# Issuing the x loads of a window-attention kernel from the ACT queue instead of SyncE

## The chip, the core and the metric

The kernel runs on one core of a Trainium2 chip. The metric is device time in microseconds, median of several runs. A run counts as fast unless it is over 1.5% above the fastest run of the same kernel; comparisons below use fast runs only. Names: PE is TensorE's matmul stream, ACT is ScalarE, DVE VectorE, POOL GpSimd, SP SyncE, which in this kernel only issues transfers. The issue time of a transfer is how long its instruction holds the queue that issues it; the transfer lands when all its data has arrived.

## The reference

Forward and backward of shifted-window attention without the shift: the image (256 x 256 pixels, 384 channels, bf16) is cut into windows of 8 x 8 = 64 tokens. The outputs are the forward result and the gradients of x, wqkv and wo.

```python
qkv = xw @ wqkv                      # xw: windows x 64 x 384
p = softmax(einsum('bqc,bkc->bqk', q, k) * 384 ** -0.5)
o = einsum('bqk,bkc->bqc', p, v) @ wo
_out, _vjp = jax.vjp(_f, x, wqkv, wo)
_grads = _vjp(grad_out)
```

## The kernel before

The loop takes 128 steps. A step handles eight windows (`QUAD` = 4 pairs) and works on three groups of windows at once: the scores and the u, v projections of one, the z and y projections of the next, and `attend` of the one before. All PSUM banks (where TensorE's products are written) are one ring of eight, handed out in turn. SP issues, per step, four loads of x (96 KB each) and four DMA transposes: `dT` and `xT` (12 blocks of 128 x 128 each), `PS` (4 blocks) and `tok` (24 blocks). POOL issues the loads of grad_out (`dq`) and the stores.

```python
ring = ctx.enter_context(tc.tile_pool(name="ring", bufs=8, space=bass.MemoryType.PSUM))
...
def load(st):
    st["xq"] = xq = grp.tile([P, QUAD, C], BF16, tag="xq", name="xq", bufs=2 * GQ + 4)
    st["dq"] = dq = qp.tile([P, QUAD, C], BF16, tag="dq", name="dq", bufs=6)
    for t in range(QUAD):
        nc.sync.dma_start(out=xq[:, t, :], in_=windows(x, st, 2 * t))
        nc.gpsimd.dma_start(out=dq[:, t, :], in_=windows(grad_out, st, 2 * t))
...
def step(c, b, a, ahead):            # cut: only the order that matters
    B(scores); ...                   # PE: sd;  then u, v projections, copied by ACT
    ...                              # softmax on DVE and ACT
    for mo in range(CK):
        A(project, 0, mo)            # PE: z from dT;  ACT copies it
    B(soft, 5); B(turn)              # SP: transpose PS<-ps
    if ahead is not None:
        load(ahead)                  # SP: four x loads;  POOL: four dq loads
    filler(1)
    C_(attend, (0, 1))               # takes all eight banks: pu, po, po, pd, pd, pw, pu, pw
    for mo in range(CK):
        A(project, 1, mo)            # PE: y;  ACT copies it
    A(to_tokens)                     # SP: transpose tok<-yz
    filler(1)
    C_(attend, (2, 3))
```

Ahead of each step stands `load_turn`, in which SP issues `dT` and `xT` of the group two steps on; its x loads were issued in the step before.

Of the kernel before, what the change touches and what calls it, by code (L numbers as in the profile page):

```python
# [11 lines left out]
BF16 = mybir.dt.bfloat16  # L12
F32 = mybir.dt.float32

P = 128
WIN = 8
WT = WIN * WIN
QUAD = 4
# [4 lines left out]
def kernel(  # L23
# [21 lines left out]
    nc = tc.nc  # L45
    _, H, W, C = x.shape
# [6 lines left out]
    grp = ctx.enter_context(tc.tile_pool(name="grp", bufs=2 * GQ + 1))  # L53
# [53 lines left out]
    def windows(ap, st, first, count=2):  # L107
        row, col = st["at"]
        return ap[0, row + WIN * first:row + WIN * (first + count), col:col + WIN, :]

    LO, HI = slice(0, WT), slice(WT, P)
    OTHER = {0: HI, WT: LO}

    def load(st):
        st["xq"] = xq = grp.tile([P, QUAD, C], BF16, tag="xq", name="xq", bufs=2 * GQ + 4)
        st["dq"] = dq = qp.tile([P, QUAD, C], BF16, tag="dq", name="dq", bufs=6)
        for t in range(QUAD):
            nc.sync.dma_start(out=xq[:, t, :], in_=windows(x, st, 2 * t))
            nc.gpsimd.dma_start(out=dq[:, t, :], in_=windows(grad_out, st, 2 * t))  # L119

    def load_turn(st):
        xq, dq = st["xq"], st["dq"]
        st["xT"] = xT = qp.tile([P, QUAD, CK, P], BF16, tag="xT", name="xT", bufs=3)
        st["dT"] = dT = qp.tile([P, QUAD, CK, P], BF16, tag="dT", name="dT")
        for src, dst in ((dq, dT), (xq, xT)):
            k = G_ON_PE if src is dq else 0
            if k < QUAD:
                nc.sync.dma_start_transpose(out=dst[:, k:].rearrange("p t m k -> p (t m) k"),
                                            in_=src[:, k:].rearrange("p t c -> p (t c)"))
# [49 lines left out]
    def over_k(ap, n=P):  # L179
        return ap.unsqueeze(2).broadcast_to([n, QUAD, WT])  # L180

    def soft(st, step):
        sd = st["sd"]
        if step == 0:
# [111 lines left out]
    def gf_group(sts):  # L296
        n = len(sts) * QUAD
        for f in range(2):
            for ma in range(CK):
                pw = ring.tile([P, C], F32, tag="r", name="pg")  # L300
                for i in range(n):
                    st, t = sts[i // QUAD], i % QUAD
                    product(pw[:], st["xq"][:, t, ma * P:(ma + 1) * P], st["UW"[f] + "q"][:, t, :], i == 0, i == n - 1)
                nc.vector.tensor_tensor(out=GF_acc[:, f, ma, :], in0=pw[:], in1=GF_acc[:, f, ma, :], op=ALU.add)  # L304
                yield

    def filler(n):
        while n and fill:
            try:
                next(fill[0])  # L310
                n -= 1
            except StopIteration:
                fill.pop(0)

    def step(c, b, a, ahead):


        def on(st):
            return (lambda f, *r: f(st, *r)) if st is not None else (lambda f, *r: None)
        C_, B, A = on(c), on(b), on(a)  # L320
        B(scores)
        B(soft, 0)
        B(uv, 0, 0)
        B(uv, 0, 1)
        B(soft, 1)
        B(uv, 1, 0)
        B(uv, 1, 1)
        B(soft, 2)
        B(soft, 3)
        B(uv, 2, 0)  # L330
        B(uv, 2, 1)
        for t in range(QUAD):
            A(grad_turn, t)
        B(uv, 3, 0)
        B(uv, 3, 1)
        B(soft, 4)
        for mo in range(CK):
            A(project, 0, mo)
        B(soft, 5)
        B(turn)  # L340
        if ahead is not None:
            load(ahead)
        filler(1)
        C_(attend, (0, 1))
        split[0] = True
        for mo in range(CK):
            A(project, 1, mo)
        A(to_tokens)
        filler(1)
        split[0] = ALL  # L350
        C_(attend, (2, 3))
# [4 lines left out]
    sts = [{"at": q, "i": i} for i, q in enumerate(quads)]  # L356
    n = len(sts)
    AHEAD = 3
    with tc.manual_schedule(engines=MANUAL):
        for i in range(min(AHEAD, n)):  # L360
            load(sts[i])
            if i < AHEAD - 1:
                load_turn(sts[i])
        held = []
        get = lambda i: sts[i] if 0 <= i < n else None
        for i in range(-1, n + 1):
            if AHEAD - 1 <= i + AHEAD - 1 < n:
                load_turn(sts[i + AHEAD - 1])
            step(get(i - 1), get(i), get(i + 1), get(i + AHEAD) if i >= 0 else None)
            if i > 0:  # L370
                held.append(sts[i - 1])
                sts[i - 1] = None
            if held and (len(held) == GQ or i == n):
                fill.append(gf_group(held))
                held = []
        split[0] = False
        filler(1 << 30)
# [62 lines left out]
```

## Time and profile before

| | before |
|---|---|
| median of 3 runs | 2007.22 us (1998.82 to 2007.71) |
| profiled span | 1997.5 us, granted clock 1.000 |
| TensorE busy | 99% |
| step of the loop | 15.2 us, 128 of them |

The lines that carry the reading stand in the prediction. The source-line views of the two longest-lived things on SP, the x loads and tok: count, then min/median/max of the issue in ns.

```profile
L118 SPq DMA_DIRECT2D xq<-in_x_dram x512: 575/600/2127, 1.2 to 1927.9; - x171
```
```profile
L167 SPq DMA_TRANSPOSE tok<-yz x128: 3862/4819/6547, 26.4 to 1951.7; - x128
```

Second, the DMA queues of the page: packets, MB, share of 16 engines. q1 is SP's, q0 POOL's, q10 ACT's, which is empty but for one load.

```profile
q1 hardware_dynamic: 943312, 270.60, 81.2%
q0 software_dynamic: 98304, 151.39, 31.1%
...
q10 hardware_dynamic: 400, 0.29, 0.0%
```

### The profile page before, as it was taken

The page shows a single profiled execution, that of the slowest core. Times are in us where ns is not written, and L with a number is a line of the kernel's source. Part 1 is how long each engine was busy: PE and PEld are TensorE (multiplying, and loading weights), DVE is VectorE, ACT ScalarE, POOL GpSimd, SP SyncE. Part 2 cuts the span into 40 slices and gives each one's busy share as a digit, 9 for nine tenths or more (in the row PEclk, how much of TensorE's full clock was granted, in tenths as well). Part 3 has the DMA queues.
Part 4 walks back from the last instruction along what each step waited for, and adds up shares of the span by engine and source line. Part 5 has one row for each costly group of instructions (what it writes and reads, how often), then busy time and mean ns, then how long its engine had stood idle before and what let it go on. Part 6 is the DMA issues. An engine that isn't in the chain of part 4 may idle for free. (4 is left out here: it accounts for less than half of the span.)

```text
span 1997.5 us, 52374 instructions
## 1 busy us (share of the span) xinstructions
PE 1967.7 (99%) x19418; PEld 1192.8 (60%) x19418; DVE 1317.2 (66%) x2979; ACT 1405.4 (70%) x3213; POOL 1122.9 (56%) x2054
## 2 busy tenths in 40 slices
PE   8899999999999999999999999999999999999998
PEld 4456656665666666566566656666665566566655
DVE  5666666666666666666666666666666666666666
ACT  5776767677777767777776777677776777776773
POOL 3555555565555556555655555565555556555643
PEclk9999999999999999999999999999999999999999
DMA  9999999999999999999999999999999999999993
GB/s 201 211 217 223 208 213 215 224 215 221 216 218 223 210 213 223 219 219 208 227 210 223 219 211 213 223 223 215 215 214 214 212 217 213 223 211 222 217 206 96
DMA packets 1042272, 425.62 MB, mean 213 GB/s; under 512 B 925792, under 2 KB 1016672, under 8 KB 1042016
## 3 DMA queue, kind: packets, MB, share of 16 engines
q1 hardware_dynamic: 943312, 270.60, 81.2%
q0 software_dynamic: 98304, 151.39, 31.1%
q8 instruction: 152, 2.49, 0.6%
q14 instruction: 104, 0.85, 0.1%
q10 hardware_dynamic: 400, 0.29, 0.0%
HBM read 101.84 MB, written 101.84 MB: 102 GB/s over the span
## 5 line engine op out<-in xcount | busy, mean ns | idle before, releaser
L292 POOL DMA_DIRECT2D out_dram<-o x256 | 139.2, 544 | 707.4 <-ACT o L264 697.4
L264 ACT CAST o<-po 128x384 bf16<-128x384 f32 x512 | 220.4, 482 | 370.0 <-PE pu L253 355.2
L304 DVE TENSOR_TENSOR GF_acc<-pg,GF_acc 128x384 f32<-128x384 f32 x258 | 144.0, 558 | 495.0 <-PE pg L145 343.8
L147 PEld LDWEIGHTS <-xT 128*128 128x128 bf16 x3072 | 291.8, 98 | 182.1
L147 PE MATMUL pj<-B_sb,xT 128*128 128x384 bf16 x1536 | 333.4, 326 | 0.0
L147 PE MATMUL pj<-AT_sb,xT 128*128 128x384 bf16 x1536 | 333.3, 326 | 0.0
L119 POOL DMA_DIRECT2D dq<-in_grad_out_dram x512 | 274.1, 547 | 66.0 <-DMA out_dram<-o 37.7
L147 PE MATMUL pj<-dT,BT_sb 128*128 128x512 bf16 x1152 | 269.7, 379 | 8.8 <-DMA dT<-dq 7.3
L145 PE MATMUL pj<-xT,A_sb 128*64 128x512 bf16 x2304 | 273.0, 380 | 1.6 <-DMA xT<-xq 1.6
L229 ACT CAST uq<-pj 128x384 bf16<-128x384 f32 x512 | 247.6, 484 | 30.6 <-PE pj L147 27.1
L229 ACT CAST vq<-pj 128x384 bf16<-128x384 f32 x512 | 249.9, 488 | 2.4 <-ACT uq L229 0.3
L145 PEld LDWEIGHTS <-xq 128*64 128x64 bf16 x3000 | 210.6, 110 | 46.3
L264 ACT CAST d<-pd 128x384 bf16<-128x384 f32 x512 | 225.2, 503 | 0.4 <-ACT o L264 0.2
L147 PEld LDWEIGHTS <-xq 128*128 128x128 bf16 x1572 | 153.6, 98 | 114.9 <-issue 0.3
L207 ACT COPY ps<-Pb 64x256 bf16<-64x256 bf16 x256 | 103.3, 403 | 149.6 <-DVE Pb L204 148.1
L163 ACT CAST yz<-pj 128x512 bf16<-128x512 f32 x384 | 206.3, 630 | 2.1 <-PE pj L145 1.8
L161 ACT CAST yz<-pj 128x512 bf16<-128x512 f32 x384 | 206.4, 639 | 1.1 <-ACT vq L229 0.7
L145 PEld LDWEIGHTS <-A_sb 128*64 128x64 bf16 x2304 | 155.7, 109 | 84.9 <-DMA xT<-xq 2.0
L147 PEld LDWEIGHTS <-BT_sb 128*128 128x128 bf16 x1152 | 111.5, 98 | 133.9 <-DMA dT<-dq 13.6
L147 PE MATMUL pg<-Uq,xq 128*128 128x384 bf16 x1032 | 181.6, 326 | 0.0
L258 PE MATMUL pd<-tok,ps 128*64 128x384 bf16 x1024 | 181.2, 344 | 0.0
L253 PE MATMUL pu<-xq,PS 64*64 64x384 bf16 x1024 | 174.9, 335 | 4.5 <-DMA PS<-ps 4.3
(67 smaller groups left out, 3382.2 us busy)
## 6 DMA issues: line engine op xcount, KB each, us to landing
xq<-in_x_dram SPq DMA_DIRECT2D x512, 96.0 KB, 4.0
dq<-in_grad_out_dram POOLq DMA_DIRECT2D x512, 96.0 KB, 3.9
out_dram<-o POOLq DMA_DIRECT2D x256, 96.0 KB, 4.2
out_dram<-o POOLq DMA_DIRECT2D x512, 48.0 KB, 4.4
out_dram<-d POOLq DMA_DIRECT2D x256, 96.0 KB, 4.4
out_dram<-d POOLq DMA_DIRECT2D x512, 48.0 KB, 4.4
dT<-dq SPq DMA_TRANSPOSE x128, 6.4
xT<-xq SPq DMA_TRANSPOSE x128, 6.7
```

The lines of the kernel that those rows point to most:

```text
L119: nc.gpsimd.dma_start(out=dq[:, t, :], in_=windows(grad_out, st, 2 * t))
L145: nc.tensor.matmul(out[h], lhsT=lhsT[:, h], rhs=rhs, start=start, stop=stop)
L147: nc.tensor.matmul(out, lhsT=lhsT, rhs=rhs, start=start, stop=stop)
L161: ENG[EV["z"][mo]](out=yz[:, mo, :, 0:4:3, :], in_=pj[:])
L163: ENG[EV["y"][mo]](out=yz[:, mo, :, 1:3, :], in_=pj[:])
L207: nc.scalar.copy(out=ps[h, :, w, :], in_=Pb[h, :, :])
L229: cp(out=dst[:, t, :], in_=pj[:])
L253: nc.tensor.matmul(at[o, :], lhsT=turned(st, lhs, t, h), rhs=st[rhs][h, t, :], **{"start": True, "stop": True, **fl})
L258: nc.tensor.matmul(pd[outer if w == 0 else 1 - outer][o, :], lhsT=st["ps"][:, t, w, :], rhs=st["tok"][:, :, t, w, :], **flags)
L264: nc.scalar.copy(out=sb[:], in_=src[outer][:])
L292: nc.gpsimd.dma_start(out=windows(dst, st, 2 * t0 + 1), in_=sb[:])
L304: nc.vector.tensor_tensor(out=GF_acc[:, f, ma, :], in0=pw[:], in1=GF_acc[:, f, ma, :], op=ALU.add)
```

## The change

SP is nearly full; ACT idles 2.14 us behind the copies of y. So the x loads of the loop move from SP to the ACT queue, behind those copies. The loads ahead of the loop stay on SP.

```diff
+    def load_x(st, queue):
+        for t in range(QUAD):
+            queue.dma_start(out=st["xq"][:, t, :], in_=windows(x, st, 2 * t))
+
     def load(st):
...
         for t in range(QUAD):
-            nc.sync.dma_start(out=xq[:, t, :], in_=windows(x, st, 2 * t))
             nc.gpsimd.dma_start(out=dq[:, t, :], in_=windows(grad_out, st, 2 * t))
...
             A(project, 1, mo)
+        if ahead is not None:
+            load_x(ahead, nc.scalar)
         A(to_tokens)
...
             load(sts[i])
+            load_x(sts[i], nc.sync)
```

More of the change, by code (lines that the diff above doesn't have):

```diff
@@ L112 @@
     OTHER = {0: HI, WT: LO}
+    def load_x(st, queue):
+        for t in range(QUAD):
+            queue.dma_start(out=st["xq"][:, t, :], in_=windows(x, st, 2 * t))
     def load(st):
-        st["xq"] = xq = grp.tile([P, QUAD, C], BF16, tag="xq", name="xq", bufs=2 * GQ + 4)
+        st["xq"] = grp.tile([P, QUAD, C], BF16, tag="xq", name="xq", bufs=2 * GQ + 4)
         st["dq"] = dq = qp.tile([P, QUAD, C], BF16, tag="dq", name="dq", bufs=6)
         for t in range(QUAD):
-            nc.sync.dma_start(out=xq[:, t, :], in_=windows(x, st, 2 * t))
             nc.gpsimd.dma_start(out=dq[:, t, :], in_=windows(grad_out, st, 2 * t))
```

## The prediction

> **What bounds the kernel now.** I read the busy table of the page first, then the waits of TensorE, then two steps of the timeline engine by engine, and last the instruction order of the changed kernel.
>
> ```profile
> PE 1967.7 (99%) x19418; PEld 1192.8 (60%) x19418; DVE 1317.2 (66%) x2979; ACT 1405.4 (70%) x3213; POOL 1122.9 (56%) x2054
> ...
> DMA  9999999999999999999999999999999999999993
> ...
> xq<-in_x_dram SPq DMA_DIRECT2D x512, 96.0 KB, 4.0
> ...
> wo_sb<-in_wo_dram ACTq DMA_DIRECT2D x1, 288.0 KB, 5.8
> ```
>
> TensorE has work in 99% of the span; only 30 us of 1997.5 are not covered, and the head and the tail of the kernel are in them. A busy TensorE could still be slow, so I checked the rate in the timeline: in the stretch of the u and v projections each group of three 128x384 products starts 0.49 us after the one before (1008.26, 1008.75, 1009.24), with nothing between. The scores start at 1007.55 and again at 1022.75: a step of the loop takes 15.2 us, there are 128, and 128 x 15.2 = 1946 us, almost the whole span. TensorE sets the pace. What could a better-fed TensorE win? Its own waits say:
>
> ```profile
> PE pj L147 <- DMA dT<-dq: 7.3, 6, 2.4
> ...
> PE pu L253 <- DMA PS<-ps: 4.3, 5, 1.6
> ...
> PE pj L145 <- DMA xT<-xq: 1.6, 1, 1.6
> ```
>
> The columns are total us, times, longest. These are the waits for the transposes that SyncE issues: 13.2 us in all, 0.7% of the run. That is the whole purse of a change that relieves SyncE, and by itself it rules out a gain of 2%.
>
> Second, SyncE is a full queue. Its timeline over one step:
>
> ```profile
> 1008.35 1.20 SPq L233 DMA_TRANSPOSE PS<-ps  x1
> 1009.59 2.79 SPq L118 DMA_DIRECT2D xq<-in_x_dram  x4
> 1012.49 5.45 SPq L167 DMA_TRANSPOSE tok<-yz  x1
> 1018.16 1.45 SPq L128 DMA_TRANSPOSE dT<-dq  x1
> 1019.79 3.23 SPq L128 DMA_TRANSPOSE xT<-xq  x1
> ```
>
> 1.20 + 2.79 + 5.45 + 1.45 + 3.23 = 14.1 us of 15.2, and the gaps are about 0.15 us each. Moreover it runs late: the y copies that tok waits for end at 1005.04 (the ACT row below), and tok is issued at 1012.49, 7.4 us later. Yet TensorE hardly feels it, as tok is not read until the step after next.
>
> Third, ScalarE (ACT), which is to take the loads. Its timeline around the new place:
>
> ```profile
> 1003.43 1.61 ACT L163 CAST yz<-pj 128x512 bf16<-128x512 f32 x3
> 1007.18 0.86 ACT L264 CAST o<-po 128x384 bf16<-128x384 f32 x2 [2.14 <-PE pu L253]
> 1007.93 0.88 ACT L264 CAST d<-pd 128x384 bf16<-128x384 f32 x2
> 1009.01 0.48 ACT L229 CAST uq<-pj 128x384 bf16<-128x384 f32 x1 [0.20 <-PE pj L147]
> ...
> 1014.83 1.61 ACT L161 CAST yz<-pj 128x512 bf16<-128x512 f32 x3
> ```
>
> Start, length, and in brackets the idle time before. Behind the three copies of y ACT idles 2.14 us, every step. The loads are put into exactly this hole, and the question of the whole case is whether they fit.
>
> **What the Trainium skill says.** "DMA: Bandwidth & Descriptors", section "Issuing engines are not separate DMA queues", says that DMAs run on the same 16 engines whoever issues them, and that issuing from several only saves sequencer time. So the change moves issue time, not transfer time; the DMA row, at 90% or more throughout, will not get lighter. "Perfetto Trace Analysis", section "DMA Instruction — HWDGE (DVE, Sync)", says that the block which generates descriptors is shared between sequencers, that an instruction waits for its lock, and that the profiled length includes this. If so, a load on ACT could wait behind a long transpose of SyncE. The trace has only one sign, and it is mild: at the very start w_sb on SyncE and wo_sb on ACT both begin at 0.74 us and take 0.45 and 0.49 us, side by side. No transpose was in flight then, so this trace doesn't decide it. The same page, section "DVE / Act Engine Instruction (TENSOR_ADD, Activation, etc)", says that the sequencer is free for the next instruction before the engine has executed the last; if that holds for an issue behind a copy, the loads start while the last y copy still runs. No row here shows it.
>
> **The change part by part.** The instruction order of both programs: TensorE, VectorE and GpSimd keep theirs; SyncE loses 125 groups of four loads (the first three groups stay); ACT gains these 500, after the third y copy and before the o copies.
>
> *Removed from SyncE:* one issue has a median of 0.600 us; four in a row took 2.58, 2.52, 3.27, 2.51, 2.98, 2.80, 2.69, 2.79 and 3.55 us in nine successive steps, 2.85 on average. SyncE then needs about 14.1 - 2.8 = 11.3 us of 15.2 and should catch up: tok would be issued right behind the y copies. The transposes' 13.2 us of waits should mostly go; I credit 5 to 10 us.
>
> *Added to ACT:* the issues. Undisturbed they are 4 x 0.6 = 2.4, with gaps about 2.5 (the best groups above); as they run on SyncE, 2.85. As they stand in the ACT stream, the o copies behind them wait.
>
> *What ACT may lose before TensorE notices.* The PSUM ring has eight banks and attend takes all eight in the order pu, po, po, pd, pd, pw, pu, pw. The scores take the first again, the first u projection the second, which is po's. That projection starts at 1008.26; the o copy that frees it runs 1007.18 to 1007.66. Slack 0.60 us. The second place is the next attend: the z copies end at 14.83 + 1.61 = 1016.44 and the third one's bank is taken by the second pu at 1016.78. Slack 0.34, plus the 0.20 that ACT idles before the first u copy: 0.54. (The 1.2 us that ACT idles before ps is no buffer, as Pb waits on ex of the same delayed stream.) So the room is 2.14 + 0.54 = 2.68 us from the end of the y copies, or 0.63 more (one y copy) if issuing begins when the last copy has been dispatched.
>
> *Sum.* Issue 2.5 in a room of 2.68: no loss. Issue 2.85, starting only at the end of y: 0.17 us a step, 125 steps, 21 us, or 1.1%. Issue 2.85 overlapped with the last y copy: no loss. Less 5 to 10 us of gain: from -10 to +16 us. The loads themselves can't be late: they are issued some 5 us earlier than SyncE does now, and are read by a transpose a step later. The xq buffers don't bind: ten of them, and the one reused was last read a step before.
>
> **The rivals.**
> 1. *ACT gets stuck behind SyncE's transposes.* SyncE's tok becomes ready at the same y copy behind which the loads stand, so both issue at the same time. For it: the long transposes (4 to 6.5 us for tok) and the shared block of the skill. If one load waits for a whole tok, ACT loses about 5 us; 5 - 0.5 gives 4 us a step and more, 25% slower. If each load is stretched to 1 us, 4 - 2.68 = 1.3 us a step, 165 us, 8% slower; at 0.8 us 3.2 - 2.68 = 0.5, 65 us, 3%. Against it: the pair at 0.74 us, and loads on SyncE itself, amid full queues, mostly near their minimum of 0.575.
> 2. *Nothing but the purse.* The loads vanish in the hole, SyncE catches up, 5 to 10 us faster: 2000 us, within 2%.
> 3. *DMA is the true co-bound.* With all engines busy, loads on a ring of their own overtake transposes, and dT or PS land later. For it the DMA row. Against it, a relieved SyncE issues the transposes earlier by more than the microsecond or two that such sharing could cost. A few us either way.
>
> **Range and chances.** Most likely the two small effects cancel: 2012 us, 5 above the median of before. The gain is capped at 13 us, and the runs of before spread from 1998.8 to 2007.7, so 1990 is the lower end. Upwards the tail is long, because a stretched issue is paid 125 times; 2110 covers an issue of up to about 0.87 us. Faster by over 2% 0.01, within 2% 0.63, slower by over 2% 0.36 (rival 1 in one of its sizes).
>
> **What would show it.** Right: the idle time of o behind pu falls from 2.14 to near 0, ACT load issues have a median near 0.6 us, SyncE shows tok within a microsecond of the y copies, the PE waits for dT and PS shrink, the step stays 15.2 us. Wrong: ACT issues of 0.8 us and more, TensorE waiting on ACT o, uq or yz in each step, a longer step. It would also be wrong if the y copies themselves moved, which the order rules out.

## The result, and the profile after

The changed kernel takes 2054.32 us (median of 4 runs, 2050.76 to 2083.18); before, on the same chips, 2005.01. The ratio is 1.0244, 95% interval 1.0208 to 1.0281: slower by 2.4%. Ratios here and below are the mean time of one kernel's fast runs over that of the other's fast runs of the same rounds, so not quite the ratio of the medians. The first profile (2083 us) is not used; the changed kernel was run once more, labelled `again`, and its profile, with a span of 2057.6 us and a granted clock of 0.997, is the one read here.

The page of the changed kernel (`again`): TensorE is no longer covered.

```profile
PE 1984.4 (96%) x19418; PEld 1196.9 (58%) x19418; DVE 1318.0 (64%) x2979; ACT 1380.9 (67%) x3213; POOL 1122.7 (55%) x2054
...
q1 hardware_dynamic: 871312, 221.41, 72.2%
q0 software_dynamic: 98304, 151.39, 33.9%
q10 hardware_dynamic: 72400, 49.48, 12.4%
```

The x loads are now on q10, as meant, but the three shares add up to 118.5% where they were 112.3%: the same bytes keep the engines longer. (The times of packets overlap, so a sum can pass 100%.) What TensorE waited for (total us, times, longest):

```profile
PE pu L256 <- DMA PS<-ps: 23.0, 19, 3.6
PE pj L150 <- ACT o L267: 21.4, 42, 1.6
PE pj L150 <- DMA dT<-dq: 9.6, 5, 4.1
```

A wait of TensorE for ACT's o copies is new, and the waits for transposes, which the change should have removed, have grown from 13.2 us to about 34 (with 1.1 us for xT). Both can be seen in single steps. ACT, then TensorE, in a step of `again`:

```profile
1182.66 1.61 ACT L166 CAST yz<-pj 128x512 bf16<-128x512 f32 x3
1183.71 3.92 ACTq L116 DMA_DIRECT2D xq<-in_x_dram  x4
1187.75 0.86 ACT L267 CAST o<-po 128x384 bf16<-128x384 f32 x2 [3.48 <-PE sd L150]
```
```profile
1186.79 0.87 PE L150 MATMUL sd<-xT,yz 128*128 128x64 bf16 x24
1188.28 0.32 PE L150 MATMUL pj<-B_sb,xT 128*128 128x384 bf16 x1 [0.62 <-ACT o L267]
```

The four loads take 3.92 us, the o copy behind them starts 3.48 us after the end of y (1184.27), and the first u projection, which needs the bank that this copy frees, starts 1.49 us after the scores instead of 0.71 (1007.55 to 1008.26 before): 0.78 us lost. Some steps on, SP is late instead:

```profile
1204.08 8.06 SPq L170 DMA_TRANSPOSE tok<-yz  x1
1212.36 4.17 SPq L131 DMA_TRANSPOSE dT<-dq  x1
1216.71 4.84 SPq L131 DMA_TRANSPOSE xT<-xq  x1
1221.71 1.44 SPq L236 DMA_TRANSPOSE PS<-ps  x1
```
```profile
1227.18 0.35 PE L261 MATMUL pd<-tok,ps 128*64 128x384 bf16 x2
1228.64 0.35 PE L256 MATMUL pu<-xq,PS 64*64 64x384 bf16 x1 [1.11 <-DMA PS<-ps]
```

Without any x load in its line, SP is still busy without a pause, as tok now takes 8.06 us and xT 4.84 (5.45 and 3.23 in the step that the prediction shows). PS comes too late for attend: pu starts 1.46 us after the product before it instead of 0.28. Over the whole trace tok's issue has a median of 6.6 us, 4.8 before:

```profile
L170 SPq DMA_TRANSPOSE tok<-yz x128: 3976/6644/9622, 26.9 to 2011.8; - x128
```

Such steps come in bursts: pu waited over 0.3 us in 17 of the 122 steps counted below. In the median SP did catch up in part: PS was issued 5.1 us after its input was ready, 8.9 before. But PS then landed 7.0 us after its issue, 4.6 before (medians).

**An account of the loss.** The profile's waits leave out the first 0.16 us or so of each stall, because the modelled end of a matmul lies after the start of its follower. So I measured in each step the distances between fixed points of TensorE's order (scores, first u, first z, attend, first pu, y, and so on) and summed what they exceed their median of before, over the same 122 steps of each trace (the fifth to the 126th):

| excess, us | u waits for o | z waits for dT | pu waits for PS | rest | all |
|---|---|---|---|---|---|
| before | 0 | 7.8 | 1.8 | 0.1 | 9.7 |
| changed (`again`) | 29.1 | 10.3 | 23.3 | 6.3 | 69.0 |

The difference, 59.3 us, is the difference of the spans (2057.6 - 1997.5 = 60.1). Half of it, 29 us, is ACT's; 24 us are later transposes. Of the rest, 6 us, the granted clock explains 5: in three stretches of 3.4 us it was 0.5, and each began 0.7 to 1.4 us after the end of one of TensorE's longest waits (2.3 to 4.1 us). One other wait of that length, 3.1 us, was followed by none. So a long wait for a transpose can cost more than its own length.

### The profile page after: what moved, and what is told of

The parts are those of the page before. It is cut to its first block, busy times and chain, and to the rows that moved or that the text cites. A ratio compares the mean times of both kernels' runs of the same rounds, so it can differ in the third digit from the quotient of the medians.

```text
span 2081.1 us, 52486 instructions
## 1 busy us (share of the span) xinstructions
PE 1994.5 (96%) x19418; PEld 1198.1 (58%) x19418; DVE 1318.0 (63%) x2979; ACT 1380.5 (66%) x3213; POOL 1123.2 (54%) x2054
## 3 DMA queue, kind: packets, MB, share of 16 engines
q10 hardware_dynamic: 72400, 49.48, 12.4%
## 5 line engine op out<-in xcount | busy, mean ns | idle before, releaser
L150 PE MATMUL pj<-dT,BT_sb 128*128 128x512 bf16 x1152 | 275.0, 385 | 21.1 <-DMA dT<-dq 18.8
L148 PE MATMUL pj<-xT,A_sb 128*64 128x512 bf16 x2304 | 278.5, 386 | 2.3 <-DMA xT<-xq 2.3
L232 ACT CAST uq<-pj 128x384 bf16<-128x384 f32 x512 | 256.3, 501 | 11.3 <-PE pj L150 7.0
L232 ACT CAST vq<-pj 128x384 bf16<-128x384 f32 x512 | 255.0, 498 | 1.5 <-ACT uq L232 0.6
```

The costliest lines, as they stand in the source:

```text
L148: nc.tensor.matmul(out[h], lhsT=lhsT[:, h], rhs=rhs, start=start, stop=stop)
L150: nc.tensor.matmul(out, lhsT=lhsT, rhs=rhs, start=start, stop=stop)
L232: cp(out=dst[:, t, :], in_=pj[:])
```

## The experiments

Two theories going in. **A:** ACT's hole is too small for four issues. **B:** loads on a queue of their own run beside the transposes and delay them. Later ones, **C** and **D**, stand where they came up. Twelve runs were made, all with correct results but for two.

**again**: the changed kernel unchanged.

> The changed kernel once more, for a profile in the fast state. Theory A (ScalarE hole too small): the four issues on ACT take 3.0 us or more from first to last against a hole of 2.68, and TensorE's wait for the o copies is the largest of its waits, 20 us or more of the some 49 that were lost. Theory B (transfers land later because three queues share the DMA engines): TensorE's waits for PS and dT together are larger than the wait for o, and all landings are 2 us later than before also in a fast run. Both expect 1.024 of before.

Measured 1.0254 (1.0212 to 1.0296). Neither theory alone: the four issues have a median of 3.06 us from first to last (mean 3.17, a tenth over 3.87), and both kinds of wait are there. The trace gives the size of the hole exactly. Grouping the steps by how long after the end of y the o copy starts, the delay of the first u is: start 2.34, delay 0.00; 2.64, 0.00; 3.00, 0.31; 3.19, 0.50; 3.44, 0.75. The room is 2.69 us, and past it each microsecond costs one.

**spread_act**: all four loads on ACT, but only two behind y. (Of the diffs below only the lines that matter are shown.)

```diff
         B(soft, 2)
+        load_x(ahead, nc.scalar, [0])       # in the idle time before ps
         B(soft, 3)
...      A(project, 0, mo)
+        load_x(ahead, nc.scalar, [1])       # behind z
...      A(project, 1, mo)
-            load_x(ahead, nc.scalar)
+            load_x(ahead, nc.scalar, [2, 3])
```

> All loads stay on the ACT queue, but one is issued in the idle time before ps, one behind the z copies, and only two behind the y copies, where 1.3 us fit into 2.14. Theory A: the waits for o go and the time returns to within 0.5% of before. Theory B: the waits for o go, but those for PS and dT stay; 1.01 to 1.025 of before.

Measured 1.0735 (1.069 to 1.078), worse than either expected. TensorE's longest waits:

```profile
PE pj L154 <- DMA dT<-dq: 72.9, 28, 6.1
PE pu L260 <- DMA PS<-ps: 52.2, 32, 5.2
```

The wait for o is gone (0.4 us), so A names a real cost, and it is not the larger danger: with ACT out of the way, the transposes come far too late. By the account of steps 131 of 166 us are waits for dT and PS; the rest, 35 us, goes with some twenty stretches at a granted clock of 0.5 (0.980 on average).

**x_on_pool** and **pool_small_act**: the x loads on POOL behind those of dq; then in addition four small loads (64 bytes a partition) on ACT behind y, to price issuing alone.

```diff
             load(ahead)
+            load_x(ahead, nc.gpsimd)
...          A(project, 1, mo)
+            nc.scalar.dma_start(out=scratch[:], in_=windows(x, ahead, 2 * t)[:, :, 0:32])   # x4, second kernel only
```

> The x loads leave SyncE but go to the GpSimd queue behind the loads of dq; ACT issues nothing, and no third queue is in use. Theory A: no slower than before, 0.995 to 1.005, as SyncE is relieved and ACT keeps its hole. Theory B, if it is the third queue: also 1.00; if it is that x no longer stands in line with the transposes: 1.01 or more with landings of transposes late as in the changed kernel.

> As x_on_pool, and four small loads (64 bytes a partition) on ACT behind the copies of y: the cost of issuing without the transfer. Theory A: slower than x_on_pool by about 1% or more, TensorE waiting for o by 10 us or more. Theory B: equal to x_on_pool within 0.4%.

Measured 1.0843 (1.0795 to 1.0892) and 1.0743 (1.0656 to 1.083). This pair missed its aim for a reason of its own. Of x_on_pool, SP's own waits:

```profile
SPq L131 <- DMA dq<-in_grad_out_dram: 464.2, 204, 6.0
```

POOL with twenty transfers a step fell behind. The first dq load of a step used to be issued 31 us before its z projection and now is 16 us before it (medians); SP stood waiting for dq, 589 us idle in all against 55 before (pauses over 0.3 us between two issues). It shows that taking the issues off SP is worth nothing when its inputs come late, and says nothing on A or B.

**x_behind_tok**: theory **C**, that the place in the step hurts, not the queue. The loads stay on SP, but behind tok.

```diff
-        if ahead is not None:
-            load_x(ahead, nc.scalar)
         A(to_tokens)
+        if ahead is not None:
+            load_x(ahead, nc.sync)
```

> The x loads stay on SyncE but stand behind tok, at the place in the program where the changed kernel has them. Theory B (a load that stands in line with the transposes costs them little, one on a queue of its own runs into them): 0.995 to 1.005 of before, landings as before. Rival C (the place in the step is what hurts, not the queue): 1.01 or more.

Measured 1.0401 (1.0353 to 1.045). The queue is not all, then: on SP itself a bad place costs 4%. SP's waits and TensorE's tell why:

```profile
SPq L131 <- DMA xq<-in_x_dram: 147.9, 115, 3.5
```
```profile
PE pu L256 <- DMA PS<-ps: 61.2, 51, 3.0
```

Behind tok, only the issue of dT lies between a load and the xT that reads it, so in 115 steps SP stands until the load has landed, and PS behind it is late. In the kernel before, tok is issued in between. It also shows that SP has nothing to spare. The changed kernel has a smaller dose of the same (45.2 us, 26 times, in `again`), because its loads, issued early but landing after a median of 7.0 us instead of 4.0, sometimes are not there when xT is due. As the main cause C fails: of the 17 steps of `again` in which pu waited over 0.3 us, 15 have no pause of SP over 0.3 us ahead of xT in themselves or in the two steps before. What sets the changed kernel apart is the transposes' own issue time: 1848 us in `again`, 1482 before, 1441 in x_behind_tok (tok alone 867, 624 and 689; PS, at 214, 189 and 228, is the exception).

**light_before** and **light_after**: half of the stores left out (out_1 wrong), to take the pressure off the transfers.

```diff
         for dst, sb, outer in stores:
+            if dst is out_1 and st["i"] > 0:
+                continue
```

> The changed kernel without the stores of d but those of the first step (out_1 wrong on purpose): about an eighth fewer bytes on the DMA engines. Theory B: waits for PS and dT fall under 10 us together, the wait for o stays near 20 us unless the issues get shorter, so some 1.00 to 1.01 of before. Theory A alone: as the changed kernel, 1.02.

> The kernel before without the same stores, as the partner of light_after: 0.99 to 1.00 of before, as only some 10 us of waits for transposes are there to be won. The difference light_after less light_before is then what the hole on ACT costs: 10 to 25 us by both theories, 50 if transfers play no part.

Measured 1.0184 (1.0143 to 1.0225) and 0.9933 (0.9899 to 0.9967); the medians differ by 49.6 us. I had written that 50 would mean that transfers play no part, but the parts don't bear this out: the part of o grew while that of the transposes went. In light_after the waits for PS and dT are gone and one is left:

```profile
PE pj L150 <- ACT o L267: 17.7, 30, 1.7
```

By the account of steps the o part is 42.5 us of 45.6; the profile names 17.7 because its list has only waits over 0.15 us, after the 0.16 us that every stall loses: 90 of the 118 stalls in the 122 steps are under 0.31 us and escape it. So the hole alone can cost 2%, and with fewer transfers it cost more than in `again`, where I had expected less. SP is now on time and issues tok at the very y copy behind which the loads stand; the fourth load of each group then has a median of 1.31 us (0.72 in `again`).

The pair shows one thing more. In light_after 63% of the x packets run beside transposing ones (the measure is explained at the table below), about as many as in `again`, and 3% in light_before. Yet SP's transposes take 1234 us of issue there against 1300 in light_before; tok alone goes from 505 to 556 us, where it goes from 624 to 867 us with all stores. So running side by side is not enough by itself: with an eighth fewer bytes (375 MB instead of 426), and an SP that is no longer full, it hardly stretched the transposes.

**half_half**, **half_half_5**, **one_act**, **three_act**: a graded dose, with 2, 1 and 3 loads of a step on ACT behind y and the others in line on SP where they were.

```diff
             load(ahead)
+            load_x(ahead, nc.sync, [0, 1])
...
-            load_x(ahead, nc.scalar)
+            load_x(ahead, nc.scalar, [2, 3])
```

> Two loads of a step in line on SyncE, two on ACT behind the y copies. Two issues take 1.3 to 1.6 us, so ACT's hole holds them. Theory A (hole) alone: 1.00. Theory B: about half of the transfer part of the loss, 1.005 to 1.015, with no wait for o.

> The kernel with two loads on ACT and two in line on SyncE again, in more rounds: 0.990 to 0.998 of before, as the first time (0.9937). If that was chance: 1.00.

> Three loads on ACT, one in line on SyncE. Three issues should take 2.0 to 2.4 us and end before the o copies are due, so no wait for o (under 5 us) by the measured room of 2.69 us. Theory A alone (the hole) then says no slower than before, 0.992 to 1.000. Theory D (loads that run beside transposes stretch them, and this passes what SyncE saves once most of the loads do it) says PS and dT come late: 1.003 to 1.02.

> One load on ACT, three in line on SyncE. Both theories: no wait for o, SyncE a little relieved, 0.994 to 1.000 of before.

Two on ACT: 0.9937 (0.9898 to 0.9975), and in five rounds 0.9944 (0.9928 to 0.996), 1992.45 us against 2002.98. This version beats both kernels, though by less than 1%. Its SP, and its TensorE's waits:

```profile
1014.61 1.19 SPq L236 DMA_TRANSPOSE PS<-ps  x1
1015.85 1.23 SPq L116 DMA_DIRECT2D xq<-in_x_dram  x2
1017.19 5.13 SPq L170 DMA_TRANSPOSE tok<-yz  x1
1022.55 2.98 SPq L131 DMA_TRANSPOSE dT<-dq  x1
1025.70 3.69 SPq L131 DMA_TRANSPOSE xT<-xq  x1
```
```profile
PE pj L150 <- DMA dT<-dq: 3.2, 2, 3.0
PE pu L256 <- DMA PS<-ps: 2.3, 2, 1.6
```

SP has caught up, as the prediction had hoped: PS is issued 2.0 us after its input is ready (median of half_half; 8.9 before). All doses in one table. "SP issue" is the issue time of SP's 512 transposes and of its x loads, summed over the trace; "beside" is the share of x packets that begin in a quarter of a microsecond in which more than 16 transposing packets begin; the last three columns are the account of steps.

| loads on ACT | ratio | SP issue: transposes + x = sum, us | beside | o | dT | PS |
|---|---|---|---|---|---|---|
| 0 (before) | 1 | 1482 + 349 = 1832 | 8% | 0 | 7.8 | 1.8 |
| 1 | 0.9945 | 1544 + 255 = 1800 | 12% | 0 | 1.6 | 0.5 |
| 2 (half_half_5) | 0.9944 | 1589 + 172 = 1760 | 28% | 0 | 0.6 | 0.8 |
| 3 | 1.0010 | 1696 + 87 = 1783 | 44% | 0.4 | 8.7 | 0.5 |
| 4 (changed) | 1.0254 | 1848 + 8 = 1856 | 63% | 29.1 | 10.3 | 23.3 |

(Intervals: 1, 0.9927 to 0.9962; 3, 0.9988 to 1.0031.) This is theory **D**. The sums of issue time fit it: each load taken out of line saves SP some 85 us and stretches the transposes by 62, 44, 107 and 152 us in turn. The first two pay, the last two don't. The time fits less well: for three loads D had asked for 1.003 to 1.02 with PS and dT late, and 1.0010 with PS on time was measured. spread_act goes with the row of 4 (70% beside, 1983 us of transposes). Three loads also settle A's part: they fit into the hole, and o costs 0.4 us. What is lost against two loads is, by the account, 13.0 us: 8.1 of dT, in two stalls early in the loop, and 4.8 of the rest, with two stretches at half the clock that began during or right after these stalls.

How the ACT issue itself behaves is in the source-line view, of one_act and of `again`:

```profile
L116 ACTq DMA_DIRECT2D xq<-in_x_dram x125: 548/548/613, 30.5 to 1911.6; - x125
```
```profile
L116 ACTq DMA_DIRECT2D xq<-in_x_dram x500: 542/642/1883, 31.8 to 1983.3; - x167
```

A lone load takes 0.548 us, in all 125 cases while SP is issuing as well: in 75 of them a transpose, for at least a part of the time, in 50 only x loads of its own. In `again` 78 of the first loads ran wholly within the issue of a transpose, and took 0.542 to 0.629 us. The first of each four takes 0.543 (median by place in the group), the second 0.646, the third 0.774, the fourth 0.715.

**act_busy**: theory A's hole without any transfer: the kernel before, and one long ACT copy behind y.

```diff
+            nc.scalar.copy(out=busy[:], in_=busy[:])      # 128 x 2900 bf16
         A(to_tokens)
```

> The kernel before, all loads on SyncE, and one long copy on ACT behind the y copies in place of the issues, so no transfer is changed. Theory A's sum: TensorE stalls in each step by the start of the o copy after the end of y less 2.69 us; with a copy of about 3 us, o starts at 3.0 to 3.2 and the step grows by 0.3 to 0.5 us, 40 to 65 us in all (1.02 to 1.033), without waits for PS or dT. If the hole is not what TensorE waits on: 1.00.

Measured 1.0027 (1.0008 to 1.0045). The copy was shorter than I had reckoned:

```profile
1009.66 1.61 ACT L166 CAST yz<-pj 128x512 bf16<-128x512 f32 x3
1011.29 2.61 ACT L352 COPY busy<-busy 128x2900 bf16<-128x2900 bf16 x1
1013.81 0.47 ACT L267 CAST o<-po 128x384 bf16<-128x384 f32 x1
```

The o copy starts 2.54 us after the end of y, inside the room of 2.69, and the account shows 0 us of o in 122 steps. So this run confirms the lower side of the room and, against my number, not the upper.

## Why the prediction was right or wrong

The time, 2054, lies in the range of 1990 to 2110; slower by over 2% was given 0.36 and "within 2%" 0.63. Most likely it had held 2012, and that the time is in the range is partly luck. The upper end was worked out from stretched issues alone, and these paid 29 us of the 59; the 24 us of later transposes stood in the sum as a gain of 5 to 10. By its own steps:

- *TensorE sets the pace, and the purse is 13 us.* Right. The best version gained 10 us, and its waits for transposes are nearly nil.
- *ACT's room of 2.68 us.* Right to 0.05, and closer only by chance. The 2.69 measured in `again` is the room of the first u, for which the prediction's slack of 0.60 gives 2.74; the first u starts 0.05 us after the end of the o copy that it waits for. The 2.68 was reckoned for another place, the second pu, and between the first pu and y there is no loss (0.5 us in all).
- *Issuing may begin when the last y copy has been dispatched, 0.63 earlier.* Right: loads start 0.06 us after the start of that copy (median), 0.56 before its end.
- *"Issue 2.85 overlapped with the last y copy: no loss."* This term failed. The issue was mis-sized, at a mean of 3.17 us instead of 2.85, and I set a mean against the room, but a step can't lend its slack to the next. The issue took 3.06 in the median and over 3.87 in a tenth of the steps, and only the steps past the room count, 55 of 122; they made 29 us.
- *"SyncE then needs about 14.1 - 2.8 = 11.3 us of 15.2 and should catch up", credit 5 to 10 us.* This failed, and it is the step I should have doubted. Per step SP's transposes alone take 1848 / 128 = 14.4 us in the changed kernel. The 2.8 us came back as longer transposes, with the loads out of the line in which they ran while the transposes paused, and now beside them (8% of their packets before, 63% now). In the median SP did come closer (tok issued 1.8 us after the y copies, 8.3 before), but instead of winning 5 to 10 us the transposes cost 24 more, in bursts.
- *"The loads themselves can't be late."* Wrong in part: SP stood waiting for them 26 times, 45.2 us in all.
- *Rival 1, a load stuck behind a whole tok.* Wrong as a mechanism: the longest single load took 1.88 us (2.35 in light_after), far from the 5 us that it would cost, and a lone load beside a transpose takes its minimum. The milder form, each load stretched, is what happened (means by place in a group of `again`: 0.55, 0.77, 0.84 and 0.88 us).
- *Rival 3, DMA as the co-bound.* Right in kind, too small in size ("a few us either way"), and my argument against it, that a relieved SP issues earlier by more than the microsecond or two that sharing costs, assumed the relief and had the cost too low: landings grew by 1.4 (dT) to 4.0 us (tok).

Open: whether the transposes are stretched in the DMA engines or where descriptors are made. A transposing packet's mean time hardly moved (26.6 ns before, 27.4 in `again`), while tok's landing went from 8.4 to 12.4 us, so the loss is between packets; no run tells more. Open also what stretches the second to fourth load of a group, the transposes or the load before. That the overlap causes the stretch, and only at full traffic, rests on the order of the doses and on the light pair; no run changes the overlap alone and leaves the place of the loads and their queue as they are.

## What to carry to other kernels

Moving transfers from a full issuing queue to an idle one frees only issue time, and if the transfers run alongside what is left, while the DMA engines are as full as here, that can take the freed time back; move a part, measure, and stop where the sum of issue times is least. Compare an insertion into an idle gap with the gap in each step, not on average: time past the gap is paid and time short of it is lost. A load needs distance from the instruction that reads it, on an in-order queue above all.

## What the Trainium skill lacked or had wrong

- "DMA: Bandwidth & Descriptors", section "Issuing engines are not separate DMA queues", says that issuing from several engines saves only the sequencer's time. It lacks that this can be negative: with four plain loads a step on ACT, SP's own 512 transposes went from 1482 to 1848 us of issue, with two to 1589. With an eighth fewer bytes on the DMA engines four loads did not do it (1300 to 1234).
- "Perfetto Trace Analysis", section "DMA Instruction — HWDGE (DVE, Sync)", describes a lock on the descriptor block that an issue waits for and that the profiled length includes. A lone ACT load showed no such wait: all 125 took between 0.548 and 0.613 us, 75 of them beside a transpose of SP. Loads right behind another on ACT were longer (medians of 0.646, 0.774 and 0.715 us by place); whether that is the lock, no run here tells.
- The same page, section "DVE / Act Engine Instruction (TENSOR_ADD, Activation, etc)", agrees with the traces that the sequencer goes on before the engine is done, but lacks the case of an issue on ACT: it began 0.06 us after the start of the copy ahead of it, 0.56 us before that copy's end.
